# DeltaNet, then a routed mixture of experts: expert tiles of 128 tokens, three sets of weight buffers, output scatters without a chain

## The chip, the core and the metric

The kernel runs on one core of a Trainium2 chip. A core has five engines with queues of their own: PE (TensorE, matrix products; its weight loads are listed apart, as PEld), DVE (VectorE), ACT (ScalarE), POOL (GpSimd) and SP (SyncE, which here issues DMAs and loads registers), and 16 DMA engines that carry what the queues issue. The metric is the device time of one execution in microseconds (us); lower is better. Times of the kernel before: 980.25, 984.8 and 983.29 us, median 983.29 us.

## The reference

Two blocks follow each other. DeltaNet attention, for 4 batches, 8 heads, 768 steps and head size 48, all in float32:

```python
k_n = k / (np.linalg.norm(k, axis=-1, keepdims=True) + 1e-06)
for t in range(S):
    kt, vt, bt = (k_n[:, :, t], v[:, :, t], beta[:, :, t, None])
    y[:, :, t] = np.einsum('bhd,bhde->bhe', q[:, :, t], state)
    v_old = np.einsum('bhde,bhd->bhe', state, kt)
    state = state + bt[:, :, :, None] * np.einsum('bhd,bhe->bhde', kt, vt - v_old)
```

Its output, as 3072 tokens of 384 numbers, goes to a mixture of 8 experts. A cosine router picks one expert for each token and gives its weight; that expert is a layer of 384 to 1024, a Relu, and a layer of 1024 to 384:

```python
logits = xn @ en.T / tau
expert_idx = np.argmax(logits, axis=1)
gate_w = probs[np.arange(N), expert_idx]
for e in range(E):
    mask = expert_idx == e
    h = np.maximum(x[mask] @ w1[e], 0.0)
    out[mask] = gate_w[mask, None] * (h @ w2[e])
```

## The kernel before, in words

**First part (to line 587).** The attention runs in chunks of 64 steps, in an order written out by hand (`tc.manual_schedule()`, lines 140 to 586). Its rows go to a table `x_dram` in DRAM (3072 rows of 384 numbers, a 385th column for the gate weight, and a last row of zeros). `route` (L422 to L484) picks the expert of each token, counts tokens per expert in `run`, and scatters each token's number into a list `idmap` in DRAM, which has one stretch per expert and was filled with N (the zero row) first. The scatters (L482) are indirect DMAs of POOL, one after the other.

**Plan of the tiles (L601 to L631).** Tokens of one expert are cut into tiles of T = 256. Since the counts are known only at run time, the program has room for the worst case: NT = 3072 / 256 + 7 = 19 tiles, always computed. Small operations on one partition of DVE work out for each tile its expert (`which`) and where its stretch of `idmap` begins (`begin`), and put both into `info`. Empty places of a tile hold N: they gather the zero row, and their output is dropped by the bounds of the scatter.

**`fetch(i)` (L634 to L650).** SP loads the tile's two numbers from `info` into registers, and issues three DMAs: the tile's token numbers `ids` (L638), the expert's `w1` (L640, 1.5 MB) and `w2` (L642, 1.5 MB). There are two buffers of each (`wt`, bufs=2). POOL then gathers the tile's rows from `x_dram` by `ids`, in two halves of 128 tokens (`xg`, L646).

**`experts(...)` (L652 to L676).** For each half, three transposes on PE (L657) turn 128 tokens into a PSUM buffer, and DVE copies them into `xT` (L658). First layer: for each of 8 blocks of 128 hidden units 3 products with 256 tokens as columns (L664), and so 24 a tile; ACT applies Relu to two blocks at a time (L666, 128x512) into `hT`. Second layer: for each half 8 products of 384 columns (L670) into one PSUM buffer; DVE multiplies by the gate weight (`y`, L673); POOL scatters the rows into `out` (L674). Transposes and second layer share two PSUM buffers (tag "one"); the first layer has three.

The weights of a product are the `lhsT` operand: each product loads 128x128 of them anew, and each is run as two passes, since the data are float32 (two records of a weight load and two of a matmul).

**What sets the order.** The loop (L678 to L683) fetches tile i + 1 ahead of the computation of tile i. This part stands outside the hand-written order: the framework's planner puts the instructions onto the engines' queues by its own account of what is ready, with the source order as priority, and adds the waits that the buffers and tiles ask for. Each queue then runs in its order. Two scatters into `out` count as writes of the same tensor, so each waits for the landing of the one before.

Of the kernel before, what the change touches and what calls it, by code (L numbers as in the profile page):

```python
# [8 lines left out]
F32 = mybir.dt.float32  # L9
I32 = mybir.dt.int32  # L10
AX = mybir.AxisListType
ALU = mybir.AluOpType
ACT = mybir.ActivationFunctionType
SP = mybir.EngineType.SP

C = 64
T = 256
Q = 32


# [1 line left out]
def kernel(  # L22
# [33 lines left out]
    nc = tc.nc  # L56
    B, H, S, D = q.shape
    NC, NP, Dm, N = S // C, H // 2, H * D, B * S
    E, _, F = moe_w1.shape
    KC, NF = Dm // 128, F // 128  # L60
    NT = N // T + E - 1
    NMAP = E * N + NT * T
    P2 = B // 2
# [6 lines left out]
    x_dram = tc.dram_tile([N + 1, Dm + 1], F32, name="x_dram")  # L70
    idmap = tc.dram_tile([NMAP, 1], I32, name="idmap")
# [4 lines left out]
    ident = cpool.tile([128, 128], F32, name="ident")  # L76
# [27 lines left out]
    ps = att.enter_context(tc.tile_pool(name="ps", bufs=1, space=bass.MemoryType.PSUM))  # L104
# [43 lines left out]
    for b in range(4):  # L148
        for i in range(2):
            for p in range(P2):  # L150
                o = (2 * b + i) * BL + p * H
# [434 lines left out]
    manual.close()  # L586
    att.close()

    ps = ctx.enter_context(tc.tile_pool(name="psm", bufs=1, space=bass.MemoryType.PSUM))

    def two():
        return ps.tile([128, 2, 512], F32, name="two", tag="two", bufs=3)

    def one(shape):
        return ps.tile(shape, F32, name="one", tag="one", bufs=2)


    wt = ctx.enter_context(tc.tile_pool(name="wt", bufs=2))
    mk = ctx.enter_context(tc.tile_pool(name="mk", bufs=2))

    thr_i = cpool.tile([1, E, N // T], I32, name="thr_i")  # L601
    nc.gpsimd.iota(thr_i, pattern=[[0, E], [T, N // T]], base=0, channel_multiplier=0)
    thr = cpool.tile([1, E, N // T], F32, name="thr")
    nc.vector.tensor_copy(thr, thr_i)
# [4 lines left out]

    nc.vector.tensor_tensor(thr, run[0:1].unsqueeze(2).broadcast_to([1, E, N // T]), thr, op=ALU.is_gt)  # L610
    tiles = cpool.tile([1, 1, E], F32, name="tiles")
# [22 lines left out]
    def fetch(i):  # L634
        e = nc.values_load(info[0:1, 0, i:i + 1], engines=(SP,), min_val=0, max_val=E - 1)
        s = nc.values_load(info[0:1, 1, i:i + 1], engines=(SP,), min_val=0, max_val=NMAP - T)
        ids = mk.tile([128, 2], I32, name="ids", tag="ids", bufs=4)
        nc.sync.dma_start(ids, idmap[bass.ds(s, T), :].rearrange("(p t) o -> p (t o)", t=2))  # L638
        w1 = wt.tile([128, KC, F], F32, name="w1", tag="w1")
        nc.sync.dma_start(w1, moe_w1[bass.ds(e, 1)].rearrange("o (c p) f -> p (o c) f", p=128))  # L640
        w2 = wt.tile([128, NF, Dm], F32, name="w2", tag="w2")
        nc.sync.dma_start(w2, moe_w2[bass.ds(e, 1)].rearrange("o (f p) m -> p (o f) m", p=128))  # L642
        xg = []
        for t in range(2):
            x = mk.tile([128, Dm + 1], F32, name="xg", tag="xg", bufs=6)
            nc.gpsimd.indirect_dma_start(  # L646
                out=x, out_offset=None, in_=x_dram[:, :],
                in_offset=bass.IndirectOffsetOnAxis(ap=ids[:, t:t + 1], axis=0))
            xg.append(x)
        return ids, w1, w2, xg  # L650

    def experts(ids, w1, w2, xg):  # L652
        xT = mk.tile([128, KC, T], F32, name="xTm", tag="xTm")
        for t in range(2):
            psX = one([128, KC, 128])
            for j in range(KC):
                nc.tensor.transpose(psX[:, j, :], xg[t][:, j * 128:(j + 1) * 128], ident)  # L657
            nc.vector.tensor_copy(xT[:, :, t * 128:(t + 1) * 128], psX)  # L658
        hT = mk.tile([128, NF, T], F32, name="hT", tag="hT")
        for f in range(0, NF, 2):  # L660
            psH = two()
            for i in range(2):
                for j in range(KC):
                    nc.tensor.matmul(psH[:, 0, i * T:(i + 1) * T], lhsT=w1[:, j, (f + i) * 128:(f + i + 1) * 128], rhs=xT[:, j, :],  # L664
                                     start=(j == 0), stop=(j == KC - 1))
            nc.scalar.activation(hT[:, f:f + 2, :], psH[:, 0].rearrange("p (i t) -> p i t", i=2), ACT.Relu)  # L666
        for t in range(2):
            psO = one([128, Dm])
            for f in range(NF):
                nc.tensor.matmul(psO, lhsT=hT[:, f, t * 128:(t + 1) * 128], rhs=w2[:, f, :],  # L670
                                 start=(f == 0), stop=(f == NF - 1))
            y = mk.tile([128, Dm], F32, name="y", tag="y", bufs=4)
            nc.vector.tensor_scalar_mul(y, psO, xg[t][:, Dm:Dm + 1])  # L673
            nc.gpsimd.indirect_dma_start(  # L674
                out=out[:, :], out_offset=bass.IndirectOffsetOnAxis(ap=ids[:, t:t + 1], axis=0),
                in_=y, in_offset=None, bounds_check=N - 1, oob_is_err=False)  # L676

    ahead = fetch(0)  # L678
    for i in range(NT):
        now = ahead  # L680
        if i + 1 < NT:
            ahead = fetch(i + 1)
        experts(*now)  # L683


# [28 lines left out]
```

## Time and profile before

| | |
|---|---|
| profiled execution, time | 983.6 us |
| its span, first to last instruction | 980.7 us |
| mean granted TensorE clock over the span | 0.824 |
| PE busy in the span | 718.4 us (73%) |
| first product of the expert stage | 535.24 us |
| PE busy, 600 to 900 us | 286.55 of 300 us |
| DMA traffic of the span | 109.57 MB |

A profile is one execution, taken on the chip; times of a row count from the start of the span. PE's records overlap, since a product's end is modelled with the time it takes through the array: the distance between starts is what a product costs in a stream. The granted clock 1.00 is 2.4 GHz, and 0.50 is 1.2 GHz. "Idle before" names what ended an engine's wait.

### The profile page before, as it was taken

The numbers are of one execution on the slowest core, as the hardware profiler recorded it, in microseconds if no ns is written. First come the engines' busy times: TensorE is split into PE (matmuls) and PEld (weight loads), VectorE is DVE, ScalarE is ACT, GpSimd is POOL, SyncE is SP. The second block draws the span as 40 slices with busy tenths as digits, with TensorE's granted clock in tenths as the row PEclk, the third lists the DMA queues.
The fourth block names the chain that finished last, engine by engine and source line by source line (L and its number), as shares of the span: only waits on it lengthen the run. The fifth ranks groups of instructions, "written<-read, shape, count | busy, mean of one in ns | idle before, by whom it ended". The sixth has DMA issues, their size and how long they took to land. (4 is left out here: it accounts for less than half of the span.)

```text
span 980.7 us, 17338 instructions
## 1 busy us (share of the span) xinstructions
PE 718.4 (73%) x7305; PEld 577.7 (59%) x7305; DVE 277.0 (28%) x727; ACT 167.0 (17%) x330; POOL 226.7 (23%) x228
## 2 busy tenths in 40 slices
PE   0534476958280699896602999999999999999995
PEld 0423475848270599785501777776666666677773
DVE  2338754738430567520310000000001001100000
ACT  0211041423120243332200101101000000001110
POOL 3742524233202403022022111111111111211100
PEclk9956596777755787676755999999999999999998
DMA  3434745474330326303006654454555444555400
GB/s 58 74 78 103 124 84 115 81 145 86 81 63 6 63 58 146 73 2 67 17 0 233 201 170 161 155 172 155 178 181 178 158 159 155 171 182 185 153 0 0
DMA packets 197903, 109.57 MB, mean 112 GB/s; under 512 B 163329, under 2 KB 186041, under 8 KB 197826
## 3 DMA queue, kind: packets, MB, share of 16 engines
q1 hardware_dynamic: 190992, 96.00, 37.1%
q0 software_dynamic: 5632, 12.24, 4.4%
q8 instruction: 57, 0.93, 0.4%
q10 hardware_dynamic: 1202, 0.23, 0.1%
q14 instruction: 20, 0.16, 0.1%
HBM read 92.56 MB, written 18.63 MB: 113 GB/s over the span
## 5 line engine op out<-in xcount | busy, mean ns | idle before, releaser
L664 PE MATMUL two<-xTm,w 128*128 128x256 f32 x912 | 204.1, 384 | 12.4 <-DVE xTm L658 12.4
L670 PE MATMUL one<-w,hT 128*128 128x384 f32 x608 | 199.2, 486 | 0.0
L664 PEld LDWEIGHTS two<-xTm,w 128*128 128x128 f32 x912 | 173.2, 192 | 40.2 <-DVE xTm L658 17.0
L670 PEld LDWEIGHTS one<-w,hT 128*128 128x128 f32 x608 | 115.5, 190 | 76.5
L673 DVE TENSOR_SCALAR y<-one,xg 128x384 f32<-128x384 f32 x38 | 23.5, 618 | 390.2 <-PE one L670 390.2
L666 ACT ACTIVATE hT<-two 128x512 f32<-128x512 f32 x76 | 45.4, 598 | 431.1 <-PE two L664 431.1
L674 POOL DMA_INDIRECT out_dram<-y,ids x38 | 38.1, 1004 | 242.1 <-DVE y L673 242.1
L290 DVE TENSOR_TENSOR tmp<-Bk,Tk 128x31 f32<-128x31 f32 (+15 forms) x186 | 74.7, 401 | 5.0
L357 PE MATMUL r<-R,W 64*64 64x48 f32 x704 | 30.5, 251 | 59.8 <-DVE R L348 59.8
L292 DVE TENSOR_TENSOR Tk<-Tk,tmp 128x31 f32<-128x31 f32 (+15 forms) x186 | 68.2, 367 | 6.4
L646 POOL DMA_INDIRECT xg<-x_dram,ids x38 | 37.3, 982 | 134.6 <-DMA ids<-idmap 103.7
L357 PEld LDWEIGHTS r<-R,W 64*64 64x64 f32 x704 | 28.2, 167 | 63.7 <-DVE R L348 59.9
L259 PE MATMUL f<-KQ 48*64 48x128 f32 x768 | 39.0, 336 | 31.2 <-DVE AP L263 31.2
L657 PE MATMUL one<-ident,xg 128*128 128x128 f32 x114 | 20.4, 290 | 54.6 <-DMA xg<-x_dram,ids 47.7
L482 POOL DMA_INDIRECT idmap<-tokid,slot_i x24 | 23.5, 981 | 129.9 <-DMA idmap<-tokid,slot_i 69.6
L259 PEld LDWEIGHTS f<-KQ 48*64 48x64 f32 x768 | 31.5, 170 | 35.0 <-DVE AP L263 32.8
L657 PEld LDWEIGHTS one<-ident,xg 128*128 128x128 f32 x114 | 13.6, 145 | 65.1 <-issue 50.7
L337 PE MATMUL r<-S,KQ 128*64 128x96 f32 x704 | 50.6, 312 | 0.0
L326 PE MATMUL f<-Wd,PI 64*64 64x32 f32 x768 | 38.4, 272 | 16.2 <-ACT PI L318 16.1
L326 PEld LDWEIGHTS f<-Wd,PI 64*64 64x64 f32 x768 | 36.9, 198 | 19.3 <-ACT PI L318 18.3
L337 PEld LDWEIGHTS r<-S,KQ 128*64 128x64 f32 x704 | 43.0, 181 | 2.4 <-issue 1.0
L247 ACT ACTIVATE KQ<-f 128x512 f32<-128x512 f32 x48 | 27.8, 597 | 88.9 <-PE f L246 88.5
(123 smaller groups left out, 653.8 us busy)
## 6 DMA issues: line engine op xcount, KB each, us to landing
w<-in_moe_w_dram SPq DMA_DIRECT2D x38, 1536.0 KB
K<-in_k_dram SPq DMA_DIRECT2D x48, 96.0 KB
Qp<-in_q_dram SPq DMA_DIRECT2D x96, 48.0 KB
Kl<-in_k_dram SPq DMA_DIRECT2D x48, 96.0 KB
V<-in_v_dram SPq DMA_DIRECT2D x48, 96.0 KB
x_dram<-xc SPq DMA_DIRECT2D x24, 192.0 KB
a_dram<-AP SPq DMA_DIRECT2D x48, 64.0 KB
Bk<-a_dram SPq DMA_DIRECT2D x6, 512.0 KB
```

The source lines that it names most:

```text
L259: nc.tensor.matmul(psG[hh][64 * g:64 * g + 64, 128 * hp:128 * hp + 128], lhsT=KQ[r, hp, g, 0, :], rhs=KQ[r, hp, g, :, :], start=True, stop ...
L290: nc.vector.tensor_tensor(tv, Bk[:, i, i + 1:Q].unsqueeze(2).broadcast_to(sh), Tk[:, i:i + 1, 0:i + 1].broadcast_to(sh), op=ALU.mult)
L292: nc.vector.tensor_tensor(Tk[:, i + 1:Q, 0:i + 1], Tk[:, i + 1:Q, 0:i + 1], tv, op=ALU.subtract)
L326: nc.tensor.matmul(psW[r, m, :], lhsT=PI[r, m, :], rhs=Wds[s][r, n + m, :], start=True, stop=True, skip_group_check=True)
L337: nc.tensor.matmul(ps1[64 * g:64 * g + 64, 2 * D * hp:2 * D * (hp + 1)], lhsT=KQs[c, p][:, hp, g, i, :], rhs=state(c, p)[:, g, hp].rearran ...
L357: nc.tensor.matmul(psZ[r, h, :], lhsT=Ws[c][r, p * H + h, :], rhs=R[r, h, :], start=True, stop=True, skip_group_check=True)
L646: nc.gpsimd.indirect_dma_start(out=x, out_offset=None, in_=x_dram[:, :], in_offset=bass.IndirectOffsetOnAxis(ap=ids[:, t:t + 1], axis=0))
L657: nc.tensor.transpose(psX[:, j, :], xg[t][:, j * 128:(j + 1) * 128], ident)
L664: nc.tensor.matmul(psH[:, 0, i * T:(i + 1) * T], lhsT=w1[:, j, (f + i) * 128:(f + i + 1) * 128], rhs=xT[:, j, :], start=(j == 0), stop=(j ...
L666: nc.scalar.activation(hT[:, f:f + 2, :], psH[:, 0].rearrange("p (i t) -> p i t", i=2), ACT.Relu)
L670: nc.tensor.matmul(psO, lhsT=hT[:, f, t * 128:(t + 1) * 128], rhs=w2[:, f, :], start=(f == 0), stop=(f == NF - 1))
L674: nc.gpsimd.indirect_dma_start(out=out[:, :], out_offset=bass.IndirectOffsetOnAxis(ap=ids[:, t:t + 1], axis=0), in_=y, in_offset=None, bou ...
```

## The change

The tile shrinks from 256 to 128 tokens (`T = 128`), and so NT = 3072 / 128 + 7 = 31. The plan's comparisons have 31 and 24 entries where they had 19 and 12. A tile is one gather, one `xT` copy, 24 products of 128 columns, 8 products of 384 columns, one `y` and one scatter. Transposes, first layer and second layer have PSUM buffers of their own (2, 4 and 2 banks); Relu takes four blocks at a time (128x512 as before). `wt` has three buffers of each weight, and the loop fetches two tiles ahead. In `fetch` the gather stands ahead of the weights. The scatters into `out` are declared free of each other.

```diff
-T = 256
+T = 128
...
-    wt = ctx.enter_context(tc.tile_pool(name="wt", bufs=2))
+    wt = ctx.enter_context(tc.tile_pool(name="wt", bufs=3))
...
-        ids = mk.tile([128, 2], I32, name="ids", tag="ids", bufs=4)
-        nc.sync.dma_start(ids, idmap[bass.ds(s, T), :].rearrange("(p t) o -> p (t o)", t=2))
+        ids = mk.tile([128, 1], I32, name="ids", tag="ids", bufs=6)
+        got = nc.sync.dma_start(ids, idmap[bass.ds(s, T), :]).ins
+        x = mk.tile([128, Dm + 1], F32, name="xg", tag="xg", bufs=4)
+        nc.gpsimd.indirect_dma_start(
+            out=x, out_offset=None, in_=x_dram[:, :],
+            in_offset=bass.IndirectOffsetOnAxis(ap=ids[:, 0:1], axis=0))
         w1 = wt.tile([128, KC, F], F32, name="w1", tag="w1")
...
-        xg = []
-        for t in range(2):
-            x = mk.tile([128, Dm + 1], F32, name="xg", tag="xg", bufs=6)
...
+    def experts(ids, w1, w2, x):
         xT = mk.tile([128, KC, T], F32, name="xTm", tag="xTm")
...
+        psX = psm.tile([128, KC, T], F32, name="psX", tag="psX", bufs=2)
+        for j in range(KC):
+            nc.tensor.transpose(psX[:, j, :], x[:, j * 128:(j + 1) * 128], ident)
+        nc.vector.tensor_copy(xT, psX)
         hT = mk.tile([128, NF, T], F32, name="hT", tag="hT")
-        for f in range(0, NF, 2):
-            psH = two()
-            for i in range(2):
+        for f in range(0, NF, 4):
+            psH = psm.tile([128, 4, T], F32, name="psH", tag="psH", bufs=4)
+            for i in range(4):
                 for j in range(KC):
-                    nc.tensor.matmul(psH[:, 0, i * T:(i + 1) * T], lhsT=w1[:, j, (f + i) * 128:(f + i + 1) * 128], rhs=xT[:, j, :],
+                    nc.tensor.matmul(psH[:, i], lhsT=w1[:, j, (f + i) * 128:(f + i + 1) * 128], rhs=xT[:, j, :],
                                      start=(j == 0), stop=(j == KC - 1))
...
+            nc.scalar.activation(hT[:, f:f + 4, :], psH, ACT.Relu)
+        psO = psm.tile([128, Dm], F32, name="psO", tag="psO", bufs=2)
+        for f in range(NF):
+            nc.tensor.matmul(psO, lhsT=hT[:, f, :], rhs=w2[:, f, :], start=(f == 0), stop=(f == NF - 1))
+        y = mk.tile([128, Dm], F32, name="y", tag="y", bufs=4)
+        nc.vector.tensor_scalar_mul(y, psO, x[:, Dm:Dm + 1])
+        put = nc.gpsimd.indirect_dma_start(
+            out=out[:, :], out_offset=bass.IndirectOffsetOnAxis(ap=ids[:, 0:1], axis=0),
+            in_=y, in_offset=None, bounds_check=N - 1, oob_is_err=False).ins
+        tc.declare_no_dep(put, group="rows", reason="each token is in one tile")
+        tc.add_to_no_dep_group("rows", put)
...
-    ahead = fetch(0)
+    ahead = [fetch(0), fetch(1)]
     for i in range(NT):
-        now = ahead
-        if i + 1 < NT:
-            ahead = fetch(i + 1)
-        experts(*now)
+        if i + 2 < NT:
+            ahead.append(fetch(i + 2))
+        experts(*ahead.pop(0))
```

## Rows read from the trace of the kernel before

**Rows 1.** The page: span; PE busy and granted clock in 40 slices (tenths).

```profile
span 980.7 us, 17338 instructions
...
PE   0534476958280699896602999999999999999995
...
PEclk9956596777755787676755999999999999999998
```

**Rows 2.** Windows: us; PE, PEld, DVE, ACT, POOL busy; clock; DMA share; GB/s.

```profile
525.00:540.00 15.00, 6.53 (x18) 4.85 (x19) 1.12 (x2) 0.00 (x0) 3.86 (x4) 0.51 1.04 390
540.00:545.00 5.00, 5.00 (x25) 4.41 (x24) 0.00 (x0) 1.20 (x2) 0.00 (x0) 1.00 0.68 234
600.00:900.00 300.00, 286.55 (x1128) 207.35 (x1127) 29.35 (x52) 31.07 (x52) 52.67 (x53) 1.00 0.51 167
```

**Rows 3.** Lines, 530 us to the end: busy, mean ns, idle before, releaser.

```profile
L664 PE MATMUL two<-xTm,w 128*128 128x256 f32 x912 | 204.1, 384 | 12.4 <-DVE xTm L658 12.4
L670 PE MATMUL one<-w,hT 128*128 128x384 f32 x608 | 199.2, 486 | 0.0
```

**Rows 4.** Timeline, last tile: start us, us, engine, line, operation, count, idle before.

```profile
946.74 0.49 PE L657 MATMUL one<-ident,xg 128*128 128x128 f32 x3
...
946.94 0.62 DVE L673 TENSOR_SCALAR y<-one,xg 128x384 f32<-128x384 f32 x1 [4.54 <-PE one L670]
947.48 0.55 DVE L658 COPY xTm<-one 128x384 f32<-128x384 f32 x1
...
948.20 0.56 DVE L658 COPY xTm<-one 128x384 f32<-128x384 f32 x1 [0.18 <-PE one L657]
...
948.82 10.63 PE L664 MATMUL two<-xTm,w 128*128 128x256 f32 x48 [0.65 <-DVE xTm L658]
...
959.28 10.48 PE L670 MATMUL one<-w,hT 128*128 128x384 f32 x32
```

**Rows 5.** Timeline: a transpose; loads with 8 columns each; two first-layer passes.

```profile
477.89 0.27 PE L409 MATMUL f<-ident,xc 128*128 128x128 f32 x1
...
478.09 0.19 PEld L419 LDWEIGHTS f<-enT,xT 128*128 128x128 f32 x1 [0.16 <-ACT xT L411]
...
478.09 1.41 PEld L419 LDWEIGHTS f<-enT,xT 128*128 128x128 f32 x12 [0.16 <-ACT xT L411]
...
560.26 0.70 PE L664 MATMUL two<-xTm,w 128*128 128x256 f32 x2 [0.65 <-DVE xTm L658]
560.36 0.41 PEld L664 LDWEIGHTS two<-xTm,w 128*128 128x128 f32 x2
```

**Rows 6.** Timeline of the start of the expert stage.

```profile
526.00 1.00 POOL L646 DMA_INDIRECT xg<-x_dram,ids  x1 [6.47 <-issue]
...
532.41 0.87 PE L657 MATMUL one<-ident,xg 128*128 128x128 f32 x3 [47.30 <-DMA xg<-x_dram,ids]
533.32 0.56 DVE L658 COPY xTm<-one 128x384 f32<-128x384 f32 x1 [39.94 <-DMA xg<-x_dram,ids]
...
535.24 12.78 PE L664 MATMUL two<-xTm,w 128*128 128x256 f32 x48 [0.65 <-DVE xTm L658]
```

**Rows 7.** DMA, 600 to 900 us: packets, MB, share; then one issuing line.

```profile
q1 hardware_dynamic: 20596, 40.92, 40.7%
q0 software_dynamic: 3392, 9.12, 10.4%
...
w<-in_moe_w_dram SPq DMA_DIRECT2D x26, 1536.0 KB
```

**Rows 8.** Waits of SP's queue, 490 us to the end: total, times, longest.

```profile
SPq L640 <- PE two L664: 192.9, 17, 12.5
```

**Rows 9.** Timeline: POOL's gather of tile 2, scatter of tile 0.

```profile
545.75 0.94 POOL L646 DMA_INDIRECT xg<-x_dram,ids  x1 [8.35 <-DMA ids<-idmap]
...
554.12 1.03 POOL L674 DMA_INDIRECT out_dram<-y,ids  x1 [6.17 <-DVE y L673]
```

**Rows 10.** Timeline: the last y.

```profile
969.80 0.62 DVE L673 TENSOR_SCALAR y<-one,xg 128x384 f32<-128x384 f32 x1 [4.54 <-PE one L670]
```

More of the change, by code (lines that the diff above doesn't have):

```diff
@@ L587 @@
     att.close()
[L589 to L595, printed above, removed]
-    wt = ctx.enter_context(tc.tile_pool(name="wt", bufs=2))
+    psm = ctx.enter_context(tc.tile_pool(name="psm", bufs=1, space=bass.MemoryType.PSUM))
+    wt = ctx.enter_context(tc.tile_pool(name="wt", bufs=3))
     mk = ctx.enter_context(tc.tile_pool(name="mk", bufs=2))
@@ L642, in fetch @@
         nc.sync.dma_start(w2, moe_w2[bass.ds(e, 1)].rearrange("o (f p) m -> p (o f) m", p=128))
-        xg = []
-        for t in range(2):
-            x = mk.tile([128, Dm + 1], F32, name="xg", tag="xg", bufs=6)
[L646 to L652, printed above, removed]
-        xT = mk.tile([128, KC, T], F32, name="xTm", tag="xTm")
[L654 to L658, printed above, removed]
+        return ids, w1, w2, x
@@ L663, in experts @@
                 for j in range(KC):
-                    nc.tensor.matmul(psH[:, 0, i * T:(i + 1) * T], lhsT=w1[:, j, (f + i) * 128:(f + i + 1) * 128], rhs=xT[:, j, :],
+                    nc.tensor.matmul(psH[:, i], lhsT=w1[:, j, (f + i) * 128:(f + i + 1) * 128], rhs=xT[:, j, :],
                                      start=(j == 0), stop=(j == KC - 1))
[L666 to L676, printed above, removed]
```

## The prediction

> **What bounds the kernel now.** I read the head of the page and its 40 slices first [rows 1]: attention and routing take the first 520 us or so, at a mixed TensorE clock, and from there to the end PE stands at nine tenths or more with the clock at 1.0. The change touches only this second stretch. The windows give it its limit [rows 2]: between 600 and 900 us PE is busy for 286.55 of 300 us at the full clock (2.4 GHz), DVE, ACT and POOL are busy for a tenth to a fifth, and the DMA engines for 0.51 of the time. So the stage is worth what PE has to stream. The grouped lines name the work [rows 3]: L664 (first layer, 912 passes of 256 columns) and L670 (second layer, 608 passes of 384); a float32 product is two passes, so 24 and 16 products in each of 19 tiles.
>
> One tile, read from the timeline [rows 4]: first layer starts at 948.82, second at 959.28, so 10.46 us; the second layer's 32 records span 10.48, of which one record's modelled tail is 0.16 (0.486 [rows 3] less the 0.3225 between starts), so 10.32 us of stream (0.3225 a pass); then from 946.74 (end of the tile before, first transpose) to 948.82 lie 2.08 us in which PE does six transposes and otherwise waits: for DVE, which first scales y (946.94), then copies the two halves of xT (947.48, 948.20). 10.46 + 10.32 + 2.08 = 22.86 us a tile. The same model gives the whole stretch back: 535.24 [rows 6] + 19 x 20.78 + 18 x 2.08 + 2.15 (half clock in the first tile, below) = 969.7, and the last y starts at 969.80 [rows 10].
>
> **The change part by part.**
>
> *Smaller tiles: fewer rows, but cheaper only if a pass of 128 columns costs half.* 19 tiles of 256 are 4864 token slots; 31 of 128 are 3968, because less padding is computed. Second layer: 8 products of 384 columns a tile, 16 x 0.3225 = 5.16 us; nothing is new there, only 31 x 16 = 496 passes in place of 608.
>
> First layer: still 48 passes a tile, now of 128 columns, and 31 x 48 = 1488 in place of 912. A pass cannot be quicker than its weight load. The trace has no float32 pass of 128 x 128 weights over 128 columns, so I bound it. From below: transposes that move 128 columns follow each other at (0.49 - 0.27) / 2 = 0.11 us [rows 4, 5]. The weight load itself: twelve loads of 128 x 128 with only 8 columns streamed after each take 1.41 us, one is 0.19, so (1.41 - 0.19) / 11 = 0.111 us apart [rows 5]. Whether load and stream lie beside each other is seen at L664: of two passes the second starts at 560.26 + 0.70 - 0.38 = 560.58, and the second of the two load records shown starts at 560.36 + 0.41 - 0.19 = 560.58 too, while that pass streams [rows 5]; and 48 passes in 10.46 us leave only their own columns' time. So the next load is in the shade of the running pass, and at 128 columns the two are about equal: I take 0.1115 us. From above: load and stream one after the other, 0.11 + 0.11 = 0.22. First layer at 0.1115: 48 x 0.1115 = 5.35, and 0.11 for the first load, that nothing hides: 5.46 us.
>
> The Trainium skill, page "TensorE: Matmul & The Clock Gate", section "Back-to-back issue gap", speaks against this: it says that in a stream of weight loads and matmuls the spacing is set by both, about 81 ns at 128 columns where its isolated figure is 56. By that ratio a pass would be an estimated 0.16 us and the total some 70 us higher than my sum. The same page of the Trainium skill, section "Part 3: Packing small matmuls — row/col tiling", says a weight load overlaps a running matmul only where the row groups differ; by that the pass would be 0.22 us, and here the trace disagrees, since L664's loads have the same rows and run beside the stream.
>
> *The gap between tiles.* There is one copy of xT now, not two, and psX, psH and psO have buffers of their own. In order y, copy, first layer, the gap is 946.74 to the end of the first copy (947.48 + 0.55) and 0.06 more: 1.35 us, three transposes included. But the queues outside the hand-ordered stretch are not in source order: tile 2's gather runs on POOL at 545.75, ahead of tile 0's scatter at 554.12, which stands before it in the source [rows 9]. Ready work of a later tile is pulled ahead where an engine would idle. With two tiles fetched ahead and two psX buffers, the transposes and the xT copy of the tile after next can go into such a gap; then the next boundary has no gap at all, no idle time for pulling anything ahead, and the one behind it has 1.35 again. So 15 gaps of 30: 20.3 us. Ends: none (0) and all (40.5). I take 15, because before, both the shared PSUM buffers and the late gather forbade it, and now neither does.
>
> *Start.* Only one gather is waited for. Before, the first half's gather is issued at 526.00, its transposes run at 532.41 and its copy starts at 533.32 and takes 0.56 [rows 6]; the first layer can follow at 533.95 instead of 535.24. The first tile runs its first few us at the half clock (0.51 until 540, 1.00 from there [rows 2]); its first layer takes 12.78 us where the last one's takes 10.63 [rows 4, 6], 2.15 more, kept.
>
> *Weights: 31 fetches of 3.15 MB in place of 19.* Now: 26 loads (13 tiles) use 40.7% of 16 engines over 300 us, 9.39 us a tile; gathers and scatters 10.4%, 31.2 us for two groups of 128 rows in each of 13 tiles and a little, 1.18 each [rows 7]. Together 10.57 us of DMA for a new tile, against 10.62 (5.46 + 5.16) and a mean gap of 0.68 on PE: 94% full. The back-to-back rate is better: 390 GB/s at 525 to 540 us [rows 2], and 3.49 MB at that rate are 8.95 us. So hidden, but with little room. The third set is what hides it: SP now holds each w1 load until PE has left the buffer (192.9 us over 17 loads [rows 8]); with two sets a tile's loads could start only in the tile before and would have to take turns with PE's release, at about 11 us a tile, which is the whole period. With three they are queued a tile earlier. The cost with this cover gone is the second rival.
>
> *Off the path, at nothing.* Scatters without their chain: POOL is busy 52.67 of 300 us [rows 2] and nothing but the end waits for them. If ids land late, gather i+2 holds back scatter i behind it on POOL; y has four buffers, so PE feels it only after some 40 us. Gathers ahead of the weights in the source: other queues. The longer comparisons on DVE before the stage lie beside the last index scatters; a few tenths at most. Relu stays 128x512, two a tile in place of four; its second half has 2.6 us of second layer to hide in.
>
> *Sum.* 533.95 + 2.15 + 31 x 10.62 + 20.3 = 885.6 for the last pass; last y 0.2 later; from y to the end 980.7 - 969.8 = 10.9 [rows 1, 10], unchanged: span 896.7. The profiled execution was 983.6 for a span of 980.7, so 2.9 lie outside: **899.6 us**. That execution is 0.3 above the median of the runs shown, which I leave out.
>
> **The rivals.**
> 1. *A gap at every boundary*, if no transposes are pulled ahead: 15 x 1.35 more, 919.9 us. For it: on PE before, strictly tile after tile. *No gap*: 879.3.
> 2. *DMA sets the pace.* If loads, gathers and scatters share badly, 11.3 to 12.1 us a tile (10.57 with 7 to 14% lost to collisions): stage end about 524 + 31 x 11.7 + 10.6, with 13.8 behind it, 911 (from 899 to 924). Against it: 390 GB/s when queued.
> 3. *Partial shade*, a pass midway between 0.1115 and 0.22: 0.054 x 1488 = 80 us more, 980: no change. For it, only that no row shows a load and a stream of equal length. This is the way of the Trainium skill's page "TensorE: Matmul & The Clock Gate", section "Back-to-back issue gap".
> 4. *Slower: the load is not in the shade once the pass is as short as the load.* Pass 0.22, 0.1085 x 1488 = 161 us more: 1061. It decides from 0.1115 + (983.6 - 899.6) / 1488 = 0.168 us a pass, or 0.154 with all gaps. Against it: the loads at L664 start with the pass before. The same page of the Trainium skill, section "Part 3: Packing small matmuls — row/col tiling", would have it so for any pass.
> 5. *The change does not do what it says*: a transpose pulled ahead of a first layer whose own x is late, or loads that wait for PE all the same, leaves PE idle and takes it off the full clock. Time open, above 940.
>
> **How the numbers follow.** Forecast 0.47; gap at every boundary 0.28; no gap 0.06; DMA 0.08; partial 0.05; slower 0.04; the last 0.02. A pass of 0.109 or 0.115 moves the forecast by -4 or +5. So 888 to 928 holds the forecast, the first rival and most of the DMA case, about 8 in 10. What a measurement of this kernel can tell is about 0.5%, 4.9 us. Faster: all of the first four and part of the partial shade, 0.92; same 0.02; slower 0.06.
>
> **What would show it.** First layer's passes at 0.11 us with the clock at 1.00, 5.46 us from first to second layer; period 10.6 and 12.0 in turn (or 11.97 always); first layer waiting for DVE xT, not for a w load; DMA share 0.8 to 0.95 in the stage. Wrong if passes are over 0.13 us apart, if first-layer loads wait for DMA w, or if the clock falls in the stage.

## The result, and the profile after

The changed kernel takes 897.34 us (median of 899.38, 895.8, 889.51 and 898.88), the one before 982.79 beside it: a ratio of 0.9117, 95% interval 0.9056 to 0.9178. The forecast was 899.6 us, in a range of 888 to 928. The profiled execution took 899.38 us for a span of 897.7.

The expert stage is where it went. From the first product of the first layer to the start of the last y, it takes 887.90 - 535.60 = 352.3 us, where before it took 969.80 - 535.24 = 434.6 [rows 6, 10]. The lines of the stage, grouped from 515 us to the end (busy us, mean ns | idle before, releaser), answer to [rows 3]:

```profile
L654 PE MATMUL psH<-xTm,w 128*128 128x128 f32 x1488 | 174.4, 277 | 10.8 <-DVE xTm L648 10.3 <-DVE y L661 0.5
...
L659 PE MATMUL psO<-w,hT 128*128 128x384 f32 x496 | 165.1, 486 | 0.0
```

The first layer has 1488 passes in place of 912 and is busy for 30 us less; the second has 496 in place of 608, at the same 486 ns a record. One pair of tiles in the timeline answers to [rows 4]:

```profile
853.25 0.82 PE L647 MATMUL psX<-ident,xg 128*128 128x128 f32 x6
...
853.45 0.62 DVE L661 TENSOR_SCALAR y<-psO,xg 128x384 f32<-128x384 f32 x1 [9.90 <-PE psO L659]
...
853.99 1.01 DVE L648 COPY xTm<-psX 128x384 f32<-128x384 f32 x2
...
854.59 5.62 PE L654 MATMUL psH<-xTm,w 128*128 128x128 f32 x48 [0.52 <-DVE xTm L648]
...
860.05 5.33 PE L659 MATMUL psO<-w,hT 128*128 128x384 f32 x16
...
865.22 4.96 PE L654 MATMUL psH<-xTm,w 128*128 128x128 f32 x43
```

Six transposes run at 853.25, those of the next tile and of the one after; DVE copies both (x2); the first layer of the next tile waits for the first copy. Then comes 860.05 - 854.59 = 5.46 us of first layer, 865.22 - 860.05 = 5.17 of second, and at 865.22 the first layer of the tile after follows with nothing between (the window cuts that row at 43 of 48). From 583.45 us on, boundaries with six transposes and boundaries with none take turns; the first three and the last have three transposes each. So 17 boundaries have the gap of 1.34 us, and 13 have none.

The windows (us; PE, PEld, DVE, ACT, POOL busy; clock; DMA share; GB/s) answer to [rows 2], and the waits of PE (total us, times, longest) with the DMA queues of 600 to 850 us to [rows 7]:

```profile
525.00:540.00 15.00, 5.27 (x30) 4.90 (x31) 0.56 (x1) 0.00 (x0) 1.95 (x2) 0.55 0.97 344
540.00:545.00 5.00, 5.00 (x32) 3.94 (x32) 0.00 (x0) 1.19 (x2) 0.00 (x0) 1.00 1.07 381
...
600.00:850.00 250.00, 244.27 (x1489) 193.71 (x1488) 23.82 (x44) 26.86 (x45) 43.62 (x44) 1.00 0.94 313
```

```profile
PE psX L647 <- DMA xg<-x_dram,ids: 49.4, 1, 49.4
...
PE psH L654 <- DVE xTm L648: 10.3, 17, 0.8
...
PE psH L654 <- DVE y L661: 0.5, 1, 0.5
```

```profile
q1 hardware_dynamic: 35117, 69.63, 81.9%
q0 software_dynamic: 2903, 8.49, 11.4%
...
out_dram<-y,ids POOLq DMA_INDIRECT x22, 7.8
xg<-x_dram,ids POOLq DMA_INDIRECT x22, 7.7
```

PE waits once for data, at the start of the stage (49.4 us, the time before the first tile). From there it waits 18 times, ahead of the first product and at the 17 boundaries with a gap: 17 times the profile names the copy of xT, and once the y. No product waits for a weight load, though the DMA engines are at 0.94 and the last column of the indirect DMAs, the median time from issue to landing, is 7.8 and 7.7 us.

How the sum of the prediction stands to the trace, in us:

| term | predicted | measured |
|---|---|---|
| first product of the stage | 533.95 | 535.60 |
| first tile, half clock | 2.15 | 542.40 - 535.60 - 5.46 = 1.34 |
| 31 tiles | 31 x 10.62 | 31 x 10.62, less 13 x 0.10 = 1.3 where the first load is hidden too |
| gaps | 15 x 1.35 = 20.3 | 17 x 1.34 = 22.8 |
| last y to the end | 10.9 | 897.7 - 887.9 = 9.8 |
| outside the span | 2.9 | 1.7 |

Of the 82.3 us by which the stage is shorter, 66.9 are passes (394.8 us before, 327.9 now), 14.7 are gaps (37.4 and 22.8) and 0.8 is the half clock of the first tile, by the same reading of both traces.

### The profile page after: what moved, and what is told of

Same layout as the page of the kernel before. It is cut to its first block, busy times and chain, and to the rows that moved or that the text cites. A ratio compares the mean times of both kernels' runs of the same rounds, so it can differ in the third digit from the quotient of the medians.

```text
span 897.7 us, 18377 instructions
## 1 busy us (share of the span) xinstructions
PE 640.2 (71%) x7748; PEld 543.3 (61%) x7748; DVE 268.5 (30%) x713; ACT 158.7 (18%) x316; POOL 212.8 (24%) x214
## 3 DMA queue, kind: packets, MB, share of 16 engines
q1 hardware_dynamic: 210000, 133.75, 52.8%
q0 software_dynamic: 4736, 10.85, 4.0%
## 4 chain that ended last, share of the span: by engine, by line
PE 50%; issue 16%; DVE 14%; DMA 12%; POOL 5%; SPq 1%; ACT 1%; POOLq 0%; DVEq 0%
PE psH L654 17%; PE psO L659 16%; DMA idmap<-tokid,slot_i 9%; DVE tmp L290 4%; DVE Tk L292 3%; PE f L326 3%; PE f L246 3%; PE r L357 2%; DVE AP L263 2%; PE f L419 2%; PE r L337 2%; PE f L259 1%; DVE xTm L648 1%; PE f L316 1%; DMA Kl<-in_k_dram 1%
## 5 line engine op out<-in xcount | busy, mean ns | idle before, releaser
L654 PEld LDWEIGHTS psH<-xTm,w 128*128 128x128 f32 x1488 | 170.9, 193 | 18.7 <-DVE xTm L648 14.5
L654 PE MATMUL psH<-xTm,w 128*128 128x128 f32 x1488 | 174.4, 277 | 10.8 <-DVE xTm L648 10.3
L659 PE MATMUL psO<-w,hT 128*128 128x384 f32 x496 | 165.1, 486 | 0.0
L659 PEld LDWEIGHTS psO<-w,hT 128*128 128x128 f32 x496 | 91.9, 190 | 57.5
L661 DVE TENSOR_SCALAR y<-psO,xg 128x384 f32<-128x384 f32 x31 | 19.2, 618 | 319.9 <-PE psO L659 319.9
L656 ACT ACTIVATE hT<-psH 128x512 f32<-128x512 f32 x62 | 37.0, 597 | 363.2 <-PE psH L654 306.3
L634 POOL DMA_INDIRECT xg<-x_dram,ids x31 | 30.1, 971 | 183.1 <-DMA ids<-idmap 109.8
L662 POOL DMA_INDIRECT out_dram<-y,ids x31 | 31.3, 1009 | 124.0 <-DVE y L661 121.2
L337 PE MATMUL r<-S,KQ 128*64 128x96 f32 x704 | 48.5, 302 | 0.7 <-issue 0.7
L647 PE MATMUL psX<-ident,xg 128*128 128x128 f32 x93 | 13.5, 278 | 49.4 <-DMA xg<-x_dram,ids 49.4
L326 PEld LDWEIGHTS f<-Wd,PI 64*64 64x64 f32 x768 | 35.1, 189 | 19.6 <-ACT PI L318 18.9
L647 PEld LDWEIGHTS psX<-ident,xg 128*128 128x128 f32 x93 | 11.4, 143 | 54.9 <-issue 52.6
```

Of the source, the lines that this page charges most:

```text
L326: nc.tensor.matmul(psW[r, m, :], lhsT=PI[r, m, :], rhs=Wds[s][r, n + m, :], start=True, stop=True, skip_group_check=True)
L337: nc.tensor.matmul(ps1[64 * g:64 * g + 64, 2 * D * hp:2 * D * (hp + 1)], lhsT=KQs[c, p][:, hp, g, i, :], rhs=state(c, p)[:, g, hp].rearran ...
L634: nc.gpsimd.indirect_dma_start(out=x, out_offset=None, in_=x_dram[:, :], in_offset=bass.IndirectOffsetOnAxis(ap=ids[:, 0:1], axis=0))
L654: nc.tensor.matmul(psH[:, i], lhsT=w1[:, j, (f + i) * 128:(f + i + 1) * 128], rhs=xT[:, j, :], start=(j == 0), stop=(j == KC - 1))
L656: nc.scalar.activation(hT[:, f:f + 4, :], psH, ACT.Relu)
L659: nc.tensor.matmul(psO, lhsT=hT[:, f, :], rhs=w2[:, f, :], start=(f == 0), stop=(f == NF - 1))
```

## The experiments

The stretch ahead of the stage varies from execution to execution: in the profiled ones of this study SP issues the first token numbers between 513.3 and 531.6 us, whichever kernel it is. So the expert stage (first product to the start of the last y, from the timeline) is what is compared, and beside it the ratio to the kernel before on the same chip:

| kernel | expert stage, us | ratio, 95% interval |
|---|---|---|
| before | 434.6 | 1 |
| changed | 352.3 | 0.9117 (0.9056 to 0.9178) |
| the same again (after_again) | 353.1 | 0.9147 (0.9104 to 0.9190) |
| one psX (e1) | 371.9 | 0.9346 (0.9293 to 0.9400) |
| 256 tokens, three sets, no chain (e3) | 434.4 | 1.0005 (0.9974 to 1.0036) |
| chained scatters (e4) | 353.1 | 0.9126 (0.9075 to 0.9177) |
| two sets (e2) | 405.1 | 0.9777 (0.9701 to 0.9852) |
| two sets, one psX (e9) | 372.4 | 0.9354 (0.9312 to 0.9395) |
| two sets, gathers earlier (e11) | 348.0 | 0.9117 (0.9066 to 0.9168) |
| 64 columns in the first layer (e5) | 376.3 | 919.45 us, once |
| half the weight traffic (e6) | 351.0 | 0.9136 (0.9101 to 0.9170) |
| early transposes (e7) | 352.7 | 0.9101 (0.9066 to 0.9136) |
| early transposes, gathers earlier (e12) | 336.9 | 0.9030 (0.8988 to 0.9072) |
| the same with two sets (e13) | 336.7 | 0.9032 (0.8984 to 0.9081) |

The theory: in this stage PE's passes and gaps are the time; all else of the change is hidden. The rival: DMA, at 0.94, sets the pace or costs PE something.

**The changed kernel again.**

> The changed kernel itself, beside the others on the same chip. Expert stage 352 us within 2, 0.91 to 0.915 of the kernel before.

It holds: 353.1 us.

**What the gaps are worth.**

```diff
-        psX = psm.tile([128, KC, T], F32, name="psX", tag="psX", bufs=2)
+        psX = psm.tile([128, KC, T], F32, name="psX", tag="psX", bufs=1)
```

> One buffer for transposed tokens (psX) instead of two, all else as in the changed kernel; nothing is left out. Theory (the gap between two tiles is left out where the planner could pull the transposes of the tile after next into the gap before): with one psX no transposes are pulled ahead, all 30 boundaries show the gap of about 1.4 us instead of 17, so 13 x 1.4 = 18 us more: 915 us. Rival (the boundary costs PE nothing, since DMA at 0.94 sets the pace): no change, 897 us.

The stage is 19.6 us longer, where 18 were expected. The wait of PE for the copy of xT comes 31 times (the first product and 30 boundaries), where the changed kernel waits 18 times:

```profile
PE psH L654 <- DVE xTm L648: 26.1, 31, 0.8
```

Every tile but the first takes 11.96 us. Had DMA set the pace, the longer gaps would have cost nothing. So the second psX is worth 19.6 us of the change's 82, and by the way that the prediction gave: the planner pulls transposes ahead.

**Fetches, sets and chain alone, with 256 tokens.**

```diff
-    wt = ctx.enter_context(tc.tile_pool(name="wt", bufs=2))
+    wt = ctx.enter_context(tc.tile_pool(name="wt", bufs=3))
...
+            tc.declare_no_dep(put, group="rows", reason="each token is in one tile")
+            tc.add_to_no_dep_group("rows", put)
...
+    ahead = [fetch(0), fetch(1)]
```

> Tiles of 256 as in the kernel before, but three sets of weight buffers, fetches two tiles ahead and unchained scatters: the change without its smaller tiles. Theory (the gain is PE's columns and gaps alone): as the kernel before, 978 to 988 us. Rival (prefetch depth or the chain was worth something): faster by over 5 us.

No change: 434.4 us, and the line of the first layer is that of [rows 3] to a fifth of a microsecond. Without the smaller tile none of it moves the time.

**The chain put back.**

```diff
-        tc.declare_no_dep(put, group="rows", reason="each token is in one tile")
-        tc.add_to_no_dep_group("rows", put)
```

> The changed kernel with the scatters into out chained again (each waits for the landing of the one before). Theory (POOL is off the path, and a scatter has a whole tile of 11 us to land): 897 us within 5. Rival (scatters now take 7.8 us to land at a DMA share of 0.94 and hold back the gathers queued behind them on POOL until x is late for PE): first transposes wait for gathered rows, over 902 us.

No change: 353.1 us, and PE waits for gathered rows only once, at the start. A scatter there lands in 6.8 us (median, 600 to 850 us), the next one goes about a tile later, and the profile names none that waits for the landing of the one before. The unchained scatters are worth nothing here.

**The third set of weights.** Here the prediction gave a reason, and the runs speak against it.

```diff
-    wt = ctx.enter_context(tc.tile_pool(name="wt", bufs=3))
+    wt = ctx.enter_context(tc.tile_pool(name="wt", bufs=2))
```

> Two sets of weight buffers instead of three, all else as in the changed kernel (PE's order is the same). What the prediction said: with two sets the loads take turns with PE's release and DMA sets the pace, 899 to 924 us. Rival: the third set hides nothing, since with two each load still has about 18 us from its release to its use and takes 5 to 6 us: 897 us, and first-layer products wait for no load.

Both times were wrong. The stage is 52.8 us longer, far more than the prediction allowed for, and that in the quickest of the four executions (945.51 us; the others took 951.13, 956.33 and 979.63). But DMA is not at its limit (its share between 600 and 700 us is 0.78), and no product waits for a load, as the rival had it. The timeline shows what it is, and the waits and a window how much:

```profile
594.09 0.37 SPq L632 DMA_DIRECT2D ids<-idmap  x1
...
603.08 0.97 POOL L634 DMA_INDIRECT xg<-x_dram,ids  x1 [7.70 <-DMA ids<-idmap]
...
603.79 0.49 PE L647 MATMUL psX<-ident,xg 128*128 128x128 f32 x3
...
608.75 0.52 PE L647 MATMUL psX<-ident,xg 128*128 128x128 f32 x3 [4.48 <-DMA xg<-x_dram,ids]
...
609.11 7.15 PE L654 MATMUL psH<-xTm,w 128*128 128x128 f32 x48
```

```profile
PE psX L647 <- DMA xg<-x_dram,ids: 93.4, 14, 48.5
```

```profile
605.00:610.00 5.00, 1.25 (x8) 1.28 (x9) 0.63 (x2) 0.00 (x0) 0.90 (x1) 0.93 1.00 349
610.00:615.00 5.00, 5.00 (x36) 5.00 (x35) 0.00 (x0) 0.60 (x1) 0.80 (x1) 0.73 0.18 61
```

At 603.79 PE transposes the tokens of the next tile, whose first layer could follow 1.3 us later. But the planner has put the transposes of the tile after ahead of it, and those wait 4.48 us for their gather. In all 93.4 - 48.5 = 44.9 us go to 13 such waits. After the wait the clock falls: PE was busy for 1.25 of 5 us, the next window has 0.73, and 48 passes take 7.15 us where 5.62 are usual. That is much like the prediction's fifth rival (a transpose pulled ahead leaves PE idle and takes it off the full clock), in a kernel that it was not named for.

Why the gather is late: SP issues in the order of its queue. Token numbers of tile i + 2 stand behind the weights of tile i + 1, and with two sets these wait until PE has left tile i - 1. The waits of SP's queue show it for w1: 185.8 us for PE's first layer, where the changed kernel has 108.2.

```profile
SPq L638 <- PE psH L654: 185.8, 29, 13.1
```

Two more stretches follow the issue. The list of 594.09 holds 0.5 KB, but POOL waits for it and issues the gather only at 603.08, 9.0 us later; the rows are there at 608.75, after 5.7 us more. Together they are 14.7 us, and a tile without a gap takes 10.5. Two runs tell this from late weights. One takes the pulled-ahead transposes away:

```diff
-    wt = ctx.enter_context(tc.tile_pool(name="wt", bufs=3))
+    wt = ctx.enter_context(tc.tile_pool(name="wt", bufs=2))
...
-        psX = psm.tile([128, KC, T], F32, name="psX", tag="psX", bufs=2)
+        psX = psm.tile([128, KC, T], F32, name="psX", tag="psX", bufs=1)
```

> Two sets of weight buffers and one psX. With two sets alone the expert stage (first product to last y) took 405.1 us, and PE waited 44.9 us for gathered rows in 13 transposes that the planner had pulled ahead. Theory (it is these transposes alone, since SP issues the token numbers behind loads that wait for a buffer; the weights themselves arrive in time): without pulled-ahead transposes the stage is that of one psX with three sets, 371.9 us within 3, about 0.935 of the kernel before, and two sets are quicker with one psX than with two. Rival (two sets leave the weights late, DMA cannot queue enough): stage over 385 us, first-layer products wait for w.

It holds: 372.4 us, the stage of three sets with one psX (371.9), and 32.7 less than with two psX. The other one leaves them in and puts token numbers and gather a tile earlier, for which `ids` and `xg` get one more buffer each:

```diff
-    def fetch(i):
+    def look(i):
...
+        return ids, x
+
+    def weights(i):
...
+    looked = [look(0), look(1), look(2)]
+    loaded = [weights(0), weights(1)]
...
+        if i + 3 < NT:
+            looked.append(look(i + 3))
+        if i + 2 < NT:
+            loaded.append(weights(i + 2))
```

> Two sets of weight buffers as in the run that took 405.1 us for the expert stage, but token numbers and gather of tile i+3 stand ahead of the weights of tile i+2 in the source, so that SP does not issue them behind loads that wait for a buffer. Theory (the third set of weights is worth something only by the token numbers it lets SP issue a tile earlier; the weights are in time with two): no transposes wait for x after the first tiles, 14 gaps, stage 325.8 + 14 x 1.44 + 1.3 = 347 us within 4, no slower than three sets. Rival (two sets leave the weights late): stage over 370 us, first-layer products wait for DMA w.

It holds: 348.0 us with two sets, 4.3 less than the changed kernel with three (14 gaps in place of 17). A list takes as long here (issued at 648.84, its gather goes at 657.87), but it is asked for a tile earlier. DMA's share from 600 to 850 us is 0.94 as well:

```profile
600.00:850.00 250.00, 244.28 (x1483) 193.47 (x1483) 23.81 (x44) 26.27 (x44) 44.30 (x45) 1.00 0.94 314
```

So the third set is worth 52.8 us as the change is written, and nothing for the weights: it lets SP reach the next tile's token numbers sooner.

**The price of a pass.**

```diff
-                    nc.tensor.matmul(psH[:, i], lhsT=w1[:, j, (f + i) * 128:(f + i + 1) * 128], rhs=xT[:, j, :],
+                    nc.tensor.matmul(psH[:, i, 0:64], lhsT=w1[:, j, (f + i) * 128:(f + i + 1) * 128], rhs=xT[:, j, 0:64],
...
+            for z in (0, 64):
+                nc.scalar.activation(hT[:, f:f + 4, z:z + 64], psH[:, :, 0:64], ACT.Relu)
```

> The first layer multiplies only the first 64 token columns of each tile (Relu copies them into both halves of hT), all else as in the changed kernel. Theory (at 128 columns the weight load, 0.111 us, and the stream, 0.109 us, are equal, and the load stays): passes stay 0.11 us apart, expert stage 352 us within 4. Rival (the load is well under the stream and the columns bind): passes 0.06 to 0.08 us apart, the stage shorter by 40 us or more, until DMA sets its pace at some 10.6 us a tile, 330 us.

Half the columns save nothing in a pass. The timeline of a first layer, first with 64 columns, then with 128 (the run with one psX):

```profile
705.68 5.57 PE L654 MATMUL psH<-xTm,w 128*128 128x64 f32 x48 [0.85 <-DVE xTm L648]
```

```profile
701.26 5.62 PE L654 MATMUL psH<-xTm,w 128*128 128x128 f32 x48 [0.85 <-DVE xTm L648]
```

The starts are 0.112 us apart in both (48 weight loads span 5.43 us in both traces, and one load is 0.19): the weight load sets the pass. The stage itself missed its 352: the planner pulled no transposes ahead here (31 waits for the copy of xT; why is open), so the run to hold it against is the one with one psX, 371.9. All periods but the first are 11.96 us in both; the 4.4 us between them lie in the first tile, where the clock stays at 0.50 longer (last section).

**Half the weight traffic.**

```diff
+        if i % 2:
+            return (ids, *kept, x)
         w1 = wt.tile([128, KC, F], F32, name="w1", tag="w1")
```

> Only tiles of even number fetch weights, the next one uses the same; half of the weight traffic is left out. Theory (DMA at 0.94 is hidden whole behind PE): expert stage 352 us within 4, the time of the changed kernel, about 0.912 of the kernel before. Rival (loads that share the memory with PE cost it something, or it waits for some of them): faster by over 5 us.

The same time within 1.3 us, 351.0, at 0.53 of DMA instead of 0.94. The 16 waits for the copy are the first product and 15 gaps, two fewer than in the changed kernel (2.7 us); its first tile takes 1.6 us longer:

```profile
PE psH L659 <- DVE xTm L653: 8.5, 16, 0.7
```

With both counted, what is left is a few tenths. DMA is hidden whole: 31 fetches of weights cost no more than 16.

**The gaps taken away.**

```diff
+        nxt = turn_in(nxt[3]) if nxt else None
         psO = psm.tile([128, Dm], F32, name="psO", tag="psO", bufs=2)
```

> Transposes and the xT copy of tile i+1 stand ahead of the second layer of tile i in the source. Theory (the 17 gaps of about 1.44 us, first load included, are all that is left to gain on PE; 31 x 0.33 us of transposes come into the stream): 31 x 10.84 + 1.3 for the half clock, stage 338 us, 14 less than the changed kernel, about 0.897 of the kernel before. Rival (DMA, 10.6 us a tile when nothing collides, takes over the pace): DMA share at 0.97 or more, first-layer products or transposes wait for DMA, stage 345 to 360 us.

Missed: 352.7 us, and a ratio like that of the changed kernel. (The profiled execution took 907.75 us, the others 890.06 to 898.0; its part ahead of the stage was long, the first token numbers came at 531.6. The stage is read in that one alone; that nothing is gained holds for the others too, by the ratio.) From the sixth tile on the period, from one first layer to the next, is 10.85 us, as expected, and PE is busy without a break. But the tiles before took 12.4 to 16.4, and their waits are for gathered rows again, this time by POOL's order:

```profile
557.00 1.03 POOL L666 DMA_INDIRECT out_dram<-y,ids  x1 [11.94 <-DVE y L665]
558.34 0.97 POOL L634 DMA_INDIRECT xg<-x_dram,ids  x1 [0.30 <-issue]
...
564.51 0.52 PE L647 MATMUL psX<-ident,xg 128*128 128x128 f32 x3 [1.79 <-DMA xg<-x_dram,ids]
```

The gather of a later tile stands behind a scatter that waits 11.94 us for its y, and runs at once when that has gone. So the gather has to be put further ahead, as in the run above with two sets. With both edits:

> Three sets, transposes and xT copy of tile i+1 ahead of the second layer of tile i, and token numbers and gather a further tile ahead. The run with the early transposes alone reached 10.85 us a tile from the sixth tile on, but lost some 15 us in the tiles before, where the transposes waited for gathered rows. Theory (with the gather a tile earlier nothing waits): 31 x 10.85 us, stage 337 us, 12 to 15 us less than the changed kernel, about 0.90 of the kernel before. Rival (DMA, now at 0.97 or more, takes over): period over 11.2 us, stage as in the changed kernel, 352 us.

It holds: 336.9 us, 16 less than the changed kernel on that chip (353.1); 0.903 of the kernel before, where the changed kernel there is at 0.9147. PE is busy all the time, at 0.95 of DMA:

```profile
600.00:850.00 250.00, 250.00 (x1544) 201.16 (x1543) 27.05 (x46) 27.46 (x46) 44.61 (x45) 1.00 0.95 321
```

The edit moves the list on SP and the gather on POOL together; which of the two was needed was not taken apart. This is the quickest of the study: 884.15 us (median of six runs, 881.52 to 889.87), beside 896.51 for the changed kernel. And two sets are enough even then:

```diff
-    wt = ctx.enter_context(tc.tile_pool(name="wt", bufs=3))
+    wt = ctx.enter_context(tc.tile_pool(name="wt", bufs=2))
```

> As the one with early transposes and the gather a further tile ahead, but with two sets of weight buffers. Theory (weights are in time with two sets, even at 10.85 us a tile): stage 337 us within 4. Rival (without a third set DMA runs dry while a load waits for its buffer, and with DMA near full that is late): stage over 345 us, first or second layer waits for DMA w.

336.7 us, the same.

## Why the prediction was right, and where it was not

**The limit and the price of a pass: right.** PE sets the stage. For the changed kernel the run with half the traffic and the one with longer gaps show it from both sides; for the kernel before, PE's 286.55 of 300 us [rows 2] and the run with 256 tokens, where more sets and deeper fetches gain nothing. The pass, taken from loads that had 8 columns behind them [rows 5], was 0.1115 and is 0.112, and with 64 columns it is 0.112 too: load and stream lie beside each other and the longer one counts. The third and fourth rivals fall with it. The Trainium skill's page "TensorE: Matmul & The Clock Gate", section "Back-to-back issue gap", gives about 81 ns in a stream where its isolated figure is 56, 1.45 times. The runs here show 0.112 us for a load of 0.111, so the load itself and nothing on top. The stream beside it would be 0.109 us, an estimate from the passes of 256 and 384 columns (10.35 / 48 = 0.2156 and 10.32 / 32 = 0.3225 before, so 0.1069 for 128 more).

**The gaps: right in kind.** Transposes are pulled ahead in pairs, at 13 boundaries; the count was 15 by the reason that every second boundary is without a gap. It fails only at the start, where the first three boundaries are single (the cause is open), and at the end. That the two psX buffers allow it is shown by the run with one. The prediction's other reason, the late gather of before, finds no support: with tiles of 256 and fetches two ahead, where transposes and second layer share PSUM buffers as before, nothing is pulled ahead (434.4 us); with two sets, where the gather is late again, the planner pulls ahead all the same, and it costs.

**The third set: the step that was wrong.** "The third set is what hides it" was said of the weights, and the cost without it was put at the second rival's 899 to 924. Without it the executions take 945.51 to 979.63, and the cause is not DMA's pace but a transpose whose rows are late. The step read one wait of SP [rows 8] as a cover for the transfer behind it, and left out what else stands in SP's queue behind that wait: the next tile's token numbers, with 14.7 us from their issue to the gathered rows. With these out of the way two sets are as quick as three, at 0.94 of DMA and more. "So hidden, but with little room" was too careful as well: 94% was forecast, 0.94 measured, and at 0.95 PE still waits for nothing.

**Scatters at nothing: right**, by the run with the chain put back. Deeper fetches gain nothing with tiles of 256; with 128 they were not taken away alone, and there, by the source, the transposes that are pulled ahead need the rows that the second fetch brings. That the longer comparisons of the plan and the order of gather and weights cost nothing was not tested by itself.

**Sizes that offset each other.** The first product came 1.65 us later than the sum had it, since the part ahead of the stage was that much slower in this execution: the first token numbers were issued at 524.27, before at 522.43. From there to the first product it is 11.33 us, before 12.81, so one gather less to wait for is worth 1.48 where 1.29 was forecast. The half clock is no steady figure either: in the second trace of the same kernel the first tile takes 0.76 us longer (14.06 against 13.30). Two gaps too few (2.5), against 1.3 for hidden loads, 0.8 for the half clock, 1.1 at the end and 1.2 outside the span. So the 0.2 us between 899.6 and 899.38 are luck; single executions of the changed kernel lie 10 us apart.

## What to carry to other kernels

A smaller tile pays where padding is large and where a pass does not fall under its weight load: read the load's spacing in a stream of narrow products, the stream's in a wide one, and take the longer. Where a planner or a hand pulls work ahead on an in-order engine, ask when its data arrive, and what stands before their small DMA in the issuing queue: a token list of 0.5 KB behind a 1.5 MB load that waits for a buffer cost 52.8 us here. One more buffer of the large one mends it, and so does an order that asks for the list a tile earlier. A DMA share of 0.95 was no bound by itself here: PE waited for nothing beside it, once lists and gathers had a tile more to land.

## What the runs showed of the hardware

Gathers land in 7.7 us (median) where DMA is at 0.94, and scatters in 7.8; before, at 0.51, a gather took 3.3 and a scatter 2.6. A token list of 0.5 KB that is issued right behind the two 1.5 MB loads of a tile lets its gather go 9.0 us later (594.09 to 603.08 with two sets). The float32 weight load of 128 x 128 sets 0.111 to 0.112 us between passes at 8, 64 and 128 columns alike. The clock of the first tile stayed low for longest in the trace with 64 columns: there PE is busy for 4.35 of 5 us from 531 and 5.00 of 5 us from 536, at a granted clock of 0.50 in both windows; it is 0.57 in the window from 541 and 1.00 from 546, while the first product came at 531.66. With 128, in the changed kernel, the first product came at 535.60, and the clock is 1.00 in the window from 540. With 128 and one psX it came at 531.64, and the clock is 0.50 in the window from 530, 0.88 from 535 and 1.00 from 540. Whether the columns make this difference, one trace with 64 cannot tell.
